# Four score banks a unit on VectorE instead of two in the second layer, and values ahead of background work, in a four-layer attention kernel

## The chip, the cores and the metric

The kernel runs on one core of a Trainium2 chip, as one launch. The metric is the device time of a launch in microseconds (us). Five engines matter here: TensorE (PE in the profile; its weight loads are PEld), ScalarE (ACT), VectorE (DVE), GpSimd (POOL) and SyncE (SP), which only issues DMAs. Each works through its own queue strictly in order; a semaphore makes one wait for another. PSUM has eight banks of 128 x 512 float32 words.

## What is computed

Four attention layers follow one another on a sequence of 2048 rows of 640 values, with 32 heads of 20 values:

```python
x = x + A(layernorm(x))   # window: key j counts for query i only if 0 <= i-j < 256
x = x + B(layernorm(x))   # every query sees every key, no mask
x = x + A(layernorm(x))
x = x + B(layernorm(x))
# A and B: softmax(q @ k.T * 20**-0.5 [masked in A]) @ v, heads joined, @ wo
```

The code counts layers from 0: layers 0 and 2 are windowed (A), layers 1 and 3 are full (B). "The second layer" is layer 1.

## The kernel before

**Units.** The queries go in four chunks of 512 (`c`), the heads in eight groups of four (`g`). A unit is one layer, chunk and group. Its scores come in banks: one bank is one block of 128 keys (`kc`) against 512 queries for one of the four heads (`j`). A full-attention unit has 16 x 4 = 64 banks, a windowed one has 12 smaller ones. Units of the four layers are interleaved in one list: the four windowed units of layer 2 that follow a chunk of layer 1 stand between units of the next chunk of layer 1. Layer 1's chunk 0 is cut into four parts by keys, because its keys appear only as layer 0 goes on.

**Tiles (ticks).** The main loop puts two or three banks together to a tile. One turn of the loop, a tick, handles one tile `t` and issues in this order:

1. TensorE: the scores of tile `t` (line 1318) into one of two sets of PSUM banks, 0 to 2 for even tiles, 3 to 5 for odd ones. So scores of `t` wait until ScalarE has read tile `t-2`.
2. ScalarE: one exponential over the tile (line 1349), written as bf16 to a `pt` buffer.
3. Background work (`pump`, then `keep_clock`): normalisation, projections, output projections, the division by the softmax sums (`t_tail`), all as generators that are advanced by a credit per tick. All of their matmuls go through the helper on line 300 or its neighbours, into PSUM bank 6 (from the end of the first stage on the only bank left for them; before it, bank 5 as well), and VectorE empties the bank (lines 323, 568, 1053, 1071, 1092). `keep_clock` fills up with matmuls whose result nobody reads (`masks,ident`), so that each tick has a least amount of TensorE work: 1.76 of its units for three banks, less in proportion for fewer.
4. TensorE: the values, that is `pt` times V of a tile two ticks back (three for windowed units), accumulated in PSUM bank 7 (line 1382). At a unit's end VectorE copies bank 7 out (line 864 and its neighbours).
5. VectorE: one step or so of the side work (below), paid from a credit of its own.
6. VectorE and GpSimd: the masks of the tile before, for windowed units (lines 1431 and 1421).

The "first stage" is what `state["early"]` marks. It ends with the last part of layer 1's chunk 0, at 433 us in the profile.

**Side work.** A few banks of a full unit don't go to ScalarE: `u.aside` lists them, and VectorE computes their exponentials with a polynomial (`t_side`). Per bank it reads the scores from PSUM as scaled integers (line 920), then per pair of banks it runs five operations on 128 x 1024 values (lines 925, 931, 936, 944, 948). In layer 1 the side bank is scored by TensorE as the third bank of a tile that then holds only two banks for ScalarE, so the number of banks that TensorE scores in a tile stays three. At the unit's end its pair is multiplied with V on line 1391. Layer 3 does the same for six banks a unit, with the scores in bank 6 (line 914) rather than in a tile. Layer 1's side work has buffers in `raw_o`, which chunk 0 no longer needs, and two outgoing buffers for finished pairs.

**Where side banks stand.** The list of tiles up to layer 3's second chunk is made ahead of the loop. Side bank number `n` of a unit may stand at the earliest `3 * n` tiles after the unit's first one, which makes tiles 0 and 3 for two banks.

Of the kernel before, what the change touches and what calls it, by code (L numbers as in the profile page):

```python
# [22 lines left out]
NT = S // P  # L23
# [3 lines left out]
NC = S // C  # L27
# [9 lines left out]
E1, E0, EA, EB = 6.520200689873914e-06 * FIX, 0.7855486869812012, -1.118533968925476, 1.5344765186309814  # L37
KA = 18
SIDE_RATE = 1.2
QA = 4  # L40

PARTS = {
# [6 lines left out]
def kernel(  # L49
# [201 lines left out]
    def pump(credit, most):  # L251
        state["credit"] = min(state["credit"] + credit, most)
        floor = 0.0
        while True:
            t = choose(state["credit"] <= floor)
            if t is None:
                break
            state["credit"] -= advance(t)
            if t not in tails:
                floor = 0.6  # L260
# [390 lines left out]
    def keep_clock():  # L651

        while cool():
            t = choose(False)
            if t is not None and state["credit"] > -0.5:
                state["credit"] -= advance(t)
                continue
            b = min(mfree, key=mfree.get)
            if state["early"] and mfree[b][0] > state["tick"]:
                break  # L660
            if mfree[b][0] > state["tick"] - (0 if state["early"] else 0):
                state["owed"] += 1
                state["heat"] += 1.0
            else:
                unread(b)
        spare = state["heat"] + state["carry"] - state["least"]
        state["carry"] = min(max(spare, 0.0), 3.0)
        state["heat"] = 0.0
# [5 lines left out]
    class Unit:  # L674
        def __init__(self, l, c, g, part=None):
            self.l, self.c, self.g, self.part = l, c, g, part
            self.windowed = l % 2 == 0
            self.aside = ()
            if self.windowed:
                sets = [(m, b0, subs, j) for m, b0, subs in window_banks(c) for j in range(4)]  # L680
            else:

                if c > 0 and (l, c, g) != (3, 1, 0):
                    self.aside = tuple((NT - 1, j) for j in ((2, 3) if l == 1 else range(4)))
                    if l == 3 and (c, g) != (NC - 1, G - 1):
                        self.aside += ((NT - 2, 0), (NT - 2, 1))
                k0, k1 = key_blocks(l, part)
                sets = [
                    (None, 0, [(kc, 0, 4, 0)], j) for kc in range(k0, k1) for j in range(4)
                    if (kc, j) not in self.aside  # L690
                ]
            n = len(sets)
            self.banks = [
                (self, j, m, b0, subs, i < 4, i >= n - 4 + len(self.aside), i == n - 1)
                for i, (m, b0, subs, j) in enumerate(sets)
            ]
# [506 lines left out]
    with tc.manual_schedule():  # L1203
# [9 lines left out]
        woven = index[1, 0, 0, PARTS[1][0]]  # L1213

        banks = [b for u in units for b in u.banks]
        tiles = []
# [4 lines left out]
        while n < last_layer:  # L1221
            size = 2 if len(tiles) % 2 and narrow(banks[n][0]) else 3
            u = banks[n][0]
            at = placed.setdefault(id(u), [])
            extra = []
            if (
                len(at) < len(u.aside) and banks[n + 1][0] is u
                and len(tiles) >= 3 * len(at) + (at or [0])[0]
            ):
                kc, j = u.aside[len(at)]  # L1230
                extra = [(u, j, "side", 0, [(kc, 0, 4, 0)], False, False, False)]
                at.append(len(tiles))
                size = 2
            for b in banks[n : n + size]:
                starts.setdefault(id(b[0]), len(tiles))
            tiles.append(banks[n : n + size] + extra)
            n += size
# [20 lines left out]
        def rate(t):  # L1258

            if t >= len(tiles):  # L1260
                return 0.45
            u = tiles[t][0][0]
            if index[u.l, u.c, u.g, u.part] < woven:
                return 1.2
            done, r = 0.0, 0.6 if state["early"] else 0.3
            for task in todo:
                done += max(task.left, 0.0)
                if task.need < len(units):
                    r = max(r, done / max(starts[id(units[task.need])] - t - 16, 1))
            return min(1.1 * r, 1.0 if u.l == 0 else 0.9)  # L1270

        last_tick[0] = len(tiles)
        wide_pt = 0
# [7 lines left out]
        while ended is None or t < ended + 8:  # L1281
# [3 lines left out]
            if t < len(tiles) or banks:  # L1285
# [67 lines left out]
                    i = k  # L1353
                for i, b in enumerate(cur):
                    pts.append((t, pt, i, b))
                state["least"] = (1.76 if state["unit"] >= woven else 1.0) * n_b / 3
                state["floor"] = 0.9 if state["unit"] >= index[1, 1, 0, None] else 0.0
                load_ahead()
                r = rate(t)
                pump(r, r + 0.1)  # L1360
                keep_clock()
            else:
                ended = t if ended is None else ended
                pump(2.0, 2.0)
# [1 line left out]
            for n in range(2 if n_b == 0 or t > closed + 1 else 0):  # L1366
# [30 lines left out]
                if end:  # L1397
# [2 lines left out]
                    closed = t  # L1400
                    break

            if n_b:
                side["credit"] = min(side["credit"] + ((SIDE_RATE if state["unit"] < index[3, NC - 1, 0, None] else 1.1) if side["late"] else 0.4), 1.3)
                side_step(False)

            if t > 0 and masked is not None:
# [71 lines left out]
```

## Time and profile before

| | us |
|---|---|
| median of three runs | 2222.56 |
| the three runs | 2214.69, 2222.56, 2223.66 |
| the profiled execution | 2214.42 |
| its span, first instruction to last | 2212.7 |
| ScalarE busy in it | 2139.9 (97%) |
| TensorE busy (matmuls, ends modelled) | 1919.8 (87%) |
| VectorE busy | 1199.8 (54%) |
| GpSimd busy | 482.5 (22%) |
| mean granted TensorE clock | 0.996 |

Busy time is the union of an engine's instructions. Two instructions that follow one another on ScalarE overlap in the records (the second starts reading while the first still writes), so the mean duration of one is longer than the time from its start to the next start; where an engine is the bound, it is this pitch that counts. In the groups of instructions the columns are line, engine, operation, tiles, shape and count, then busy time, mean ns of one, and idle time of the engine just before them with what ended it. The list of waits has, for each engine and line, what it waited for, the total in us, the number of times and the longest. The table by stretches has, for each engine, its busy time in the stretch and its number of instructions.

Four stretches of the profile are used below: up to 478 us (layers 0 and 1, chunk 0), 478 to 1272 us (layer 1's chunks 1 to 3 with the windowed units of layer 2 between them), 1272 to 1570 us (layer 3's first chunk, first part, with the last windowed units, then its second part) and 1570 us to the end (layer 3).

### The profile page before, as it was taken

Reading aid. Unit: us, or ns where it says so; the run is one execution under the profiler, and the core shown is the slowest. Engines: PE = TensorE matmul, PEld = TensorE weight load, DVE = VectorE, ACT = ScalarE, POOL = GpSimd, SP = SyncE. Lnnn points to the kernel's source line nnn. Section 1 sums busy time; section 2 is a strip of 40 time slices with the busy share of each in tenths; the row PEclk is TensorE's granted clock in tenths of the full one; section 3 lists DMA queues with packets and bytes.
Section 4 is the critical chain, followed back from the end, with each engine's and each line's share of the span. In section 5 each row is a group of like instructions: output and inputs, shape, how many; then the busy total and the mean of one; then the engine's idle time right before and its main releaser. Section 6 shows DMA issues by size and latency. Waiting matters only on the chain.

```text
span 2212.7 us, 70085 instructions
## 1 busy us (share of the span) xinstructions
PE 1919.8 (87%) x30415; PEld 756.1 (34%) x30415; DVE 1199.8 (54%) x2190; ACT 2139.9 (97%) x1734; POOL 482.5 (22%) x950
## 2 busy tenths in 40 slices
PE   8889998988888888888888888888888888888888
PEld 4444443333333333333333433342332222222222
DVE  6656564434445454444554533532467767767774
ACT  7889899999999999999999999999999999999998
POOL 6664545200231114301143112511000000000000
PEclk9999999999999999999999999999999999999999
DMA  6233323421211223112230123122121111111100
GB/s 200 74 99 91 88 81 93 102 78 45 74 41 33 71 60 97 33 34 66 66 104 24 48 72 100 36 57 63 54 62 35 32 32 44 32 32 35 49 24 16
DMA packets 88404, 137.09 MB, mean 62 GB/s; under 512 B 20766, under 2 KB 63486, under 8 KB 88094
## 3 DMA queue, kind: packets, MB, share of 16 engines
q1 hardware_dynamic: 68878, 79.43, 13.0%
q0 software_dynamic: 19216, 53.17, 8.1%
q8 instruction: 238, 3.90, 0.7%
q14 instruction: 72, 0.59, 0.1%
HBM read 99.52 MB, written 27.79 MB: 58 GB/s over the span
## 4 chain that ended last, share of the span: by engine, by line
ACT 52%; PE 21%; issue 18%; DVE 6%; DMA 1%; POOL 1%; ACTq 0%; DVEq 0%; POOLq 0%
ACT pt L1349 51%; PE ps L300 12%; PE ps L1318 5%; PE ps L1382 2%; DVE on L1092 1%; DVE st L323 1%; DVE pt L1431 1%; DMA wqk<-in_B_wqkv_dram 1%; PE ps L1088 1%; PE ps L437 0%; DVE on L864 0%; DVE x_sb L568 0%; DVE raw_o L920 0%; POOL pt L1421 0%; DVE xnT L323 0%
## 5 line engine op out<-in xcount | busy, mean ns | idle before, releaser
L1349 ACT ACTIVATE pt<-ps 128x1536 bf16<-128x1536 f32 (+2 forms) x1657 | 2104.3, 1456 | 41.8 <-PE ps L1318 32.1
L1318 PE MATMUL ps<-qt,kt 32*128 32x512 bf16 x3960 | 544.6, 384 | 91.4 <-ACT pt L1349 82.9
L300 PE MATMUL ps<-masks,ident 128*32 128x512 bf16 x5844 | 510.2, 387 | 117.8 <-ACT pt L1349 68.5
L1382 PE MATMUL ps<-pt,vt 128*21 128x512 bf16 x3908 | 397.6, 383 | 1.9 <-issue 1.0
L1318 PEld LDWEIGHTS <-kt 32*128 32x128 bf16 x3960 | 163.4, 91 | 546.4 <-issue 531.0
L300 PEld LDWEIGHTS <-ident 128*32 128x32 bf16 x5844 | 165.3, 94 | 349.9 <-issue 336.7
L1421 POOL TENSOR_SCALAR_AFFINE_SELECT pt<-pt 128x256 bf16<-128x256 bf16 (+2 forms) x505 | 213.8, 445 | 189.0 <-ACT pt L1349 183.5
L300 PE MATMUL ps<-xnT,wqk 128*32 128x512 bf16 x3320 | 224.6, 383 | 15.7 <-DVE st L323 4.0
L323 DVE CAST st<-ps 128x512 bf16<-128x512 f32 x134 | 92.7, 692 | 234.0 <-PE ps L300 230.4
L920 DVE TENSOR_SCALAR xnT<-ps 128x512 int32<-128x512 f32 x136 | 93.6, 688 | 134.1 <-PE ps L914 124.6
L300 PE MATMUL ps<-wop,on 128*32 128x320 bf16 x3712 | 159.8, 301 | 7.1 <-DVE x_sb L568 4.0
L1431 DVE TENSOR_TENSOR pt<-pt,masks 128x512 bf16<-128x512 bf16 (+4 forms) x267 | 112.4, 436 | 96.8 <-ACT pt L1349 94.6
L1382 PEld LDWEIGHTS <-vt 128*21 128x21 bf16 x3912 | 104.8, 91 | 126.1 <-issue 94.1
L300 PEld LDWEIGHTS <-on 128*32 128x32 bf16 x5760 | 113.5, 95 | 74.2 <-issue 51.1
L1318 PE MATMUL ps<-qa,ka 32*128 32x384 bf16 (+2 forms) x1408 | 114.7, 275 | 27.5 <-ACT pt L1349 24.4
L568 DVE TENSOR_TENSOR x_sb<-x_sb,ps 128x320 bf16<-128x320 bf16 x120 | 58.3, 486 | 146.8 <-PE ps L300 146.6
L300 PE MATMUL ps<-wv,xnT 128*32 128x320 bf16 x2560 | 115.2, 301 | 8.3 <-DVE on L1092 2.2
L1092 DVE TENSOR_TENSOR on<-on,ps 128x512 bf16<-128x512 bf16 x128 | 86.3, 684 | 57.9 <-PE ps L1088 56.7
L300 PEld LDWEIGHTS <-wqk 128*32 128x32 bf16 x3320 | 77.1, 95 | 114.4 <-issue 61.9
L864 DVE CAST on<-ps 128x512 bf16<-128x512 f32 x112 | 77.0, 687 | 57.0 <-PE ps L1391 32.6
L536 POOL DMA_DIRECT2D k_d<-st x75 | 43.0, 573 | 233.2 <-DVE st L323 223.2
L404 POOL TENSOR_SCALAR rstd<-mv 128x4 f32<-128x4 f32 x15 | 3.7, 248 | 382.6 <-DVE mv L391 374.4
(100 smaller groups left out, 1537.5 us busy)
## 6 DMA issues: line engine op xcount, KB each, us to landing
vt<-v_d SPq DMA_DIRECT2D x48, 336.0 KB
kt<-k_d SPq DMA_DIRECT2D x192, 80.0 KB
wqk<-in_B_wqkv_dram POOLq DMA_DIRECT2D x80, 160.0 KB, 3.4
wqk<-in_A_wqkv_dram POOLq DMA_DIRECT2D x70, 160.0 KB, 3.6
k_d<-st POOLq DMA_DIRECT2D x75, 128.0 KB, 2.6
q_d<-st POOLq DMA_DIRECT2D x75, 128.0 KB, 2.2
qt<-q_d SPq DMA_DIRECT2D x384, 20.0 KB
v_d<-vs POOLq DMA_DIRECT2D x16, 336.0 KB, 3.0
```

The source lines that it names most:

```text
L300: nc.tensor.matmul(out_[r], lhsT=lhsT[:, r], rhs=rhs, start=start, stop=stop)
L323: nc.vector.tensor_copy(out=out_, in_=in_)
L536: nc.gpsimd.dma_start(out=dst, in_=staging.pop())
L568: nc.vector.tensor_tensor(out=xv, in0=had, in1=yp, op=ALU.add)
L864: nc.vector.tensor_copy(out=oT, in_=op)
L920: V.tensor_scalar(out=xi.bitcast(I32)[:, i * C : (i + 1) * C], in0=side["psum"], scalar1=SCALE * LOG2E * FIX, scalar2=-127.0 * FIX, op0=AL ...
L1092: nc.vector.tensor_tensor(out=oT, in0=oT, in1=zb, op=ALU.mult)
L1318: nc.tensor.matmul(sp[:, i, col * P : (col + qn) * P], lhsT=u.k(kc, j), rhs=u.q(j, q0, qn), start=True, stop=True,)
L1349: nc.scalar.activation(out=pt[:, i:k, b0 * P :], in_=sp[:, i:k, b0 * P :], func=ACT.Exp, scale=SCALE,)
L1382: nc.tensor.matmul(op[32 * j : 32 * j + VW, q0 * P : (q0 + qn) * P], lhsT=u.v(kc, j), rhs=pg[:, i, col * P : (col + qn) * P], start=(first ...
L1421: nc.gpsimd.affine_select(out=v, in_=v, compare_op=ALU.is_gt if later else ALU.is_ge, fill=0.0, base=0, pattern=[[0, k - i], [-1 if later ...
L1431: nc.vector.tensor_tensor(out=pt_[:, i:k, cols], in0=pt_[:, i:k, cols], in1=mv_, op=ALU.mult)
```

## The change

Three edits stand in the diff. Layer 1's later chunks list four banks a unit as aside, not two: all four heads of the last key block. They may stand at tiles 0, 3, 9 and 12 of the unit at the earliest, and the credit that paces the side work there rises from 0.4 to 0.7 a tick; layer 3's numbers stay. The background work of a tick is put into a function, `background`, that is called at the old place in the first stage only; from its end on it is called after the values of the tick.

```diff
+SIDE_AT = (0, 3, 9, 12)
...
                 if c > 0 and (l, c, g) != (3, 1, 0):
-                    self.aside = tuple((NT - 1, j) for j in ((2, 3) if l == 1 else range(4)))
+                    self.aside = tuple((NT - 1, j) for j in range(4))
...
-                and len(tiles) >= 3 * len(at) + (at or [0])[0]
+                and len(tiles) >= SIDE_AT[len(at)] + (at or [0])[0]
...
+        def background(t, n_b):
+
+            state["least"] = (1.76 if state["unit"] >= woven else 1.0) * n_b / 3
+            state["floor"] = 0.9 if state["unit"] >= index[1, 1, 0, None] else 0.0
+            r = rate(t)
+            pump(r, r + 0.1)
+            keep_clock()
...
-                state["least"] = (1.76 if state["unit"] >= woven else 1.0) * n_b / 3
-                state["floor"] = 0.9 if state["unit"] >= index[1, 1, 0, None] else 0.0
                 load_ahead()
-                r = rate(t)
-                pump(r, r + 0.1)
-                keep_clock()
+                if state["early"]:
+                    background(t, n_b)
             else:
                 ended = t if ended is None else ended
                 pump(2.0, 2.0)
...
+            if n_b and not state["early"]:
+                background(t, n_b)
             if n_b:
-                side["credit"] = min(side["credit"] + ((SIDE_RATE if state["unit"] < index[3, NC - 1, 0, None] else 1.1) if side["late"] else 0.4), 1.3)
+                side["credit"] = min(side["credit"] + ((SIDE_RATE if state["unit"] < index[3, NC - 1, 0, None] else 1.1) if side["late"] else 0.7), 1.3)
                 side_step(False)
```

The omitted stretch ahead of the last edit holds the loop over the values (line 1366 on in the kernel before).

## The prediction

> **What bounds the kernel now.** I read the busy times first, then a table of four stretches, then ScalarE's timeline, then what TensorE waited for.
>
> ```profile
> PE 1919.8 (87%) x30415; PEld 756.1 (34%) x30415; DVE 1199.8 (54%) x2190; ACT 2139.9 (97%) x1734; POOL 482.5 (22%) x950
> ```
>
> ScalarE is the bound, and the table by stretches says where:
>
> ```profile
> 430.00:478.00 48.00, 40.25 (x562) 15.02 (x563) 13.67 (x25) 47.98 (x37) 9.08 (x13) 1.00 0.30 83
> 478.00:1272.00 794.00, 680.17 (x10967) 278.13 (x10959) 384.86 (x745) 786.19 (x620) 169.60 (x317) 1.00 0.21 58
> 1272.00:1570.00 298.00, 254.74 (x4075) 105.65 (x4068) 102.41 (x212) 293.95 (x219) 71.44 (x129) 0.99 0.24 67
> 1570.00:2200.00 630.00, 549.23 (x7051) 170.95 (x7050) 440.51 (x609) 626.77 (x466) 0.00 (x0) 1.00 0.12 35
> ```
>
> After the length come busy PE, PEld, DVE, ACT, POOL. In 478:1272, where the side banks change, ScalarE is busy 786.2 of 794 us (99%) and VectorE 384.9 (48%). So work taken from ScalarE shortens the stretch, if TensorE delivers scores fast enough. The price of a bank comes from the pitch, start to start, not from durations, since exponentials overlap:
>
> ```profile
> 1492.23 39.06 ACT L1349 ACTIVATE pt<-ps 128x1536 bf16<-128x1536 f32 x29 [0.39 <-PE ps L1318]
> ```
>
> ```profile
> 552.10 1.11 ACT L1349 ACTIVATE pt<-ps 128x1024 bf16<-128x1024 f32 x1
> ```
>
> ```profile
> 553.00 1.55 ACT L1349 ACTIVATE pt<-ps 128x1536 bf16<-128x1536 f32 x1
> ```
>
> Columns: start, length, then the group. 29 three-bank exponentials back to back take 39.06 us; less one duration (1.55) that is 28 pitches of 1.34. Undisturbed ones in the records are 1.333 apart. The two-bank one starts 0.90 before its successor; undisturbed ones give 0.905. A bank taken from a tile saves 1.333 - 0.905 = **0.428 us**, less than the 482 ns by which the mean durations differ (1553 and 1071).
>
> Third, TensorE's slack: its waits in 478:1272.
>
> ```profile
> PE ps L1318 <- ACT pt L1349: 55.4, 170, 0.7
> PE ps L300 <- DVE st L323: 14.2, 47, 0.6
> PE ps L300 <- ACT pt L1349: 10.4, 28, 0.7
> PE ps L300 <- DVE on L1092: 7.9, 16, 0.8
> ```
>
> It waited 65.8 us (55.4 + 10.4) for ScalarE to free score banks. That is what it can give when ScalarE gets faster: 8% of the stretch, so TensorE is a close second. The waits for VectorE (st, on and smaller ones) are losses in its queue.
>
> **Part 1, two more banks a unit.** There are 24 such units (3 chunks x 8 groups), so 48 banks move. The instruction order of the changed kernel agrees: 50 three-bank exponentials fewer, 47 two-bank ones more, two wide ones of 2048 columns more in layer 3 (pitch 1.757). ScalarE: 50 x 1.333 - 47 x 0.905 - 2 x 1.757 = **-20.6 us**, all in 478:1272 but for the wide ones.
>
> Added to VectorE: 48 x 0.69 (line 920) and, for each of 24 pairs, 0.69 + 0.70 + 1.22 + 1.21 + 0.68 (lines 925, 931, 936, 944, 948) = 33 + 108 = 141 us, which takes its stretch to (385 + 141) / 773 = 68%. That lies beside ScalarE as long as VectorE's queue empties bank 6 and the side banks in time. TensorE: scores and values are the same in number; 17 unread fillers (of 1461) go, since a two-bank tile asks for less; the granted clock is 1.00 in 478:1272 now, and I price so few at nothing. POOL and SP get no instruction more.
>
> What a short tile costs: TensorE has 0.43 us less for that tick. In 478:1272 pitches exceed the undisturbed ones by 20.3 us, of which 17.7 us lie in a two-bank tile or the three tiles after it (sums over the records). That would be 0.37 us for each of today's 48, nearly the whole saving. But these tiles stand at a unit's start, where the tails of the unit before run and values catch up two groups a tick. The new ones stand at tiles 9 and 12. Over the 24 units TensorE's waits for ScalarE per three tiles, from the unit's first side bank, are on average 0.18, 0.24, 0.32, 0.38, 0.50, 0.50, 0.38 us: from the ninth tile on 1.76, against 0.86 for two short tiles. Bounds: 0 (all absorbed) to +17.7 (like today's). I take **+5**, 0.1 each, nearer to the mid-unit row, since that is where they stand; not zero, because single units have under 0.5 there.
>
> Third suspect, the pace: in the changed order each second pair is finished about 6 tiles ahead of its values (line 1391), so nothing waits there. Side banks are read in time today: of 48 reads, 19 found VectorE idle, and no wait of TensorE on line 920 shows in this stretch.
>
> VectorE's longer queue: records of background between scores and values hold 34.3 us of waits for VectorE in 144 of 451 cases in 478:1272. If they grow with VectorE's load (0.65 to 0.86 us a tile in the two orders, a third more), that is +11 us of TensorE's time, against 66 us of slack. Bounds: 0 to +11. I take **+2**, because most of it falls where TensorE would wait for ScalarE anyway.
>
> A rule that speaks against the part. In 478:1570, k_d's DMA issues on POOL took 0.56 us on average (30 with no side operation beside them) and 0.62, up to 1.03 (10 beside one). The Trainium skill (SBUF — State Buffer, Who interferes with whom) says that VectorE and GpSimd share a port pair, which a VectorE operation with two SBUF inputs or in a two-port mode holds for its whole length while the other blocks fully. By the row, twice the side work costs POOL 0.05 us on some ten issues more; by the rule each could wait up to a whole operation. POOL is 21% busy there, and I price it at nothing.
>
> **Part 2, values ahead of background.** From 433 us on. It adds no instruction. What stands behind the values is now the background; what stands behind a waiting background matmul is now only the next scores. Gain: a background matmul that waits for VectorE to empty bank 6 does so after the values (0.3 to 0.4 us later), so that part of the wait is filled. Cutting each wait by the length of the values behind it removes, from the records, 23.4 us of TensorE's time in 478:1272, 7.7 in 1272:1570 and 5.5 later. That is worth ScalarE's time only where it stood idle or late: 20.3 us in 478:1272, about 7 and 9 in the others; of the 33 single delays over 0.3 us after 478, 18 have VectorE waits of 0.4 or more in TensorE's queue just before. Bounds: 0 to -12 us (a third of 36). I take **-5**.
>
> Cost: values may now wait for their own masks or exponentials. Comparing, record by record, when each group's `pt` was ready with when the background ahead of it began, 12 of 893 groups would have waited, 5.2 us together (POOL masks 6, VectorE masks 5, 1.9 us of it at the very end). Bounds 0 to +5; I take **+1**. The copies of bank 7 now stand ahead of the background's on VectorE: a gain for the next unit's values, which start two ticks later anyway, at nothing. k_d's and q_d's DMAs on POOL leave up to 0.4 us later; loads are issued units ahead, at nothing.
>
> **Sum.** -20.6 + 5 + 2 - 5 + 1 = **-17.6 us**. Against the profiled execution: 2214.4 - 17.6 = 2196.8, span about 2195. The profile lies at the lower end of four executions (2214.42, 2214.69, 2222.56, 2223.66; mean 2218.8); from their mean I get **2201**.
>
> **Rivals.**
>
> (a) *TensorE becomes the bound in short tiles.* The new short tiles lose what today's lose, 17.7 us, and values ahead gives little: -20.6 + 17.7 - 2 = -5, so about 2214. For it: 87% busy TensorE, zero slack in some units' starts. Against: the slack at tiles 9 to 21.
>
> (b) *Slower: bank 6 behind VectorE.* The side steps of 1.22 us stand ahead of the copies that free bank 6; TensorE waits in order, and scores come late. The price passes the saving when the waits for VectorE exceed TensorE's remaining slack, 65.8 - 20.6 = 45 us, by 20.6; to be 11 us slower they must grow by about 77 us, over 0.5 us in each of the 144 cases that wait now. Then about 2230. For it: 141 us more on VectorE. Against: 1570:2200, where VectorE is busier still (440.5 of 630, 70%) and ScalarE stays at 626.8; though there is less background there.
>
> (c) *Values ahead is worth more than I take.* The whole -12, short tiles absorbed: -20.6 - 12 + 3 = -30, about 2189.
>
> (d) *The edit doesn't move the work.* The built order excludes this: it has 50 three-bank exponentials fewer and 48 operations like line 920's more, and the values now stand ahead of the background in most ticks.
>
> **How the numbers follow.** Forecast (2193 to 2209) 0.65; (a) 0.15; (c) 0.12; (b) 0.08. The range leaves out (b) and the far end of (c): **2186 to 2216**. A measurement can tell about 0.5% (11 us) from no change: faster means below 2211.4. The forecast and (c) lie below it, and a little of (a): faster **0.80**; the rest of (a): same **0.13**; (b): slower **0.07**.
>
> **What would show it.** In 478:1272 (then some 18 us shorter) ScalarE still 98 to 99% busy, 104 or so two-bank exponentials, about 96 operations on line 920's successor; TensorE's wait for ScalarE down from 65.8 towards 50; its waits for VectorE not above today's, as values ahead cuts them by more than the load adds; 1570:2200 shorter by 1 to 3 us. Wrong if ScalarE's idle time before exponentials grows by over 10 us (a), or if TensorE's waits for VectorE double (b).

## The result, and the profile after

| | before | after |
|---|---|---|
| median of 22 runs each, us | 2218.03 | 2227.67 |
| lowest to highest | 2214.63 to 2224.43 | 2219.20 to 2234.89 |
| the profiled execution | 2214.42 | 2221.95 |
| its span | 2212.7 | 2219.7 |
| mean granted TensorE clock | 0.996 | 0.991 |

The ratio is **1.004, with an interval of [1.0031, 1.0049]**: 9 us slower, where 17.6 us less were forecast. The forecast, its range and its sign were wrong; the time lies nearest to rival (b), 2230.

The busy line of the page after, and its costliest group:

```profile
PE 1928.6 (87%) x30347; PEld 746.5 (34%) x30347; DVE 1334.8 (60%) x2358; ACT 2125.6 (96%) x1733; POOL 486.2 (22%) x950
L1358 ACT ACTIVATE pt<-ps 128x1536 bf16<-128x1536 f32 (+2 forms) x1654 | 2086.6, 1433 | 59.2 <-PE ps L1327 47.9
```

The work moved as the diff says: VectorE is busy 135 us more, ScalarE 14 us less, and yet the span is longer. ScalarE now stands idle 47.9 us waiting for scores (line 1327). The same group before, with 32.1 us (line 1318):

```profile
L1349 ACT ACTIVATE pt<-ps 128x1536 bf16<-128x1536 f32 (+2 forms) x1657 | 2104.3, 1456 | 41.8 <-PE ps L1318 32.1
```

The stretches of after from 478 us on:

```profile
478.00:1272.00 794.00, 682.64 (x10818) 270.03 (x10815) 506.31 (x895) 766.32 (x615) 168.48 (x310) 0.98 0.21 56
1272.00:1570.00 298.00, 256.10 (x4116) 103.50 (x4113) 113.08 (x228) 295.17 (x222) 76.14 (x136) 1.00 0.26 70
1570.00:2200.00 630.00, 548.25 (x7062) 170.00 (x7060) 442.58 (x609) 626.97 (x465) 0.00 (x0) 1.00 0.13 36
```

In 478:1272 ScalarE is busy 766.3 us (96.5%; 786.2 before), VectorE 506.3 (384.9) and the clock is 0.98 (1.00). The other stretches are nearly as they were. What TensorE waited for in 478:1272 after the change:

```profile
PE ps L1327 <- ACT pt L1358: 37.5, 115, 0.6
PE ps L301 <- DVE st L324: 12.8, 20, 1.7
PE ps L301 <- DVE on L1093: 11.8, 31, 0.9
PE ps L301 <- DVE x_sb L569: 7.3, 16, 1.6
PE ps L301 <- ACT pt L1358: 6.6, 22, 0.7
...
PE ps L438 <- DVE xn L418: 5.7, 4, 2.1
PE ps L301 <- DVE rT L1072: 5.4, 12, 1.5
```

Its waits for ScalarE fell from 65.8 to 44.1 us. Of its waits for VectorE those on `st` became fewer (47 to 20), but the longest went from 0.6 to 1.7 us, and those on `x_sb` (2.6 us before), `xn` (none) and `rT` (1.9) grew. ScalarE's own waits in the same stretch, first before, then after:

```profile
ACT pt L1349 <- PE ps L1318: 6.1, 18, 0.8
```

```profile
ACT pt L1358 <- PE ps L1327: 24.2, 58, 1.3
```

Four times as much: 18 us, nearly all that the shorter exponentials gave.

**Floor and excess.** To compare runs I took "layer 1's stretch" between two fixed VectorE copies of bank 7 (the 64th and the 120th of 160, about 493 to 1410 us). Its *floor* is what ScalarE would take without a delay: each exponential of the stretch times the undisturbed pitch of its width (1.333 and 0.905 us for three and two banks, and likewise for the narrow ones). The *excess* is what the pitches exceed it by. A delay of over 0.05 us is put to *clock* if it overlaps a time of half clock, to *VectorE* if TensorE waited for VectorE for at least half of it between 2 us before the start of the exponential ahead and the time when the late one was due, and else to *busy* TensorE. The rule is mine and splits mixed cases crudely: with only the 2 us right before the late start, VectorE / clock / busy would be 17.8 / 9.7 / 21.6 after and 12.3 / 3.1 / 8.9 before. Floor, excess and the clock's part don't depend on that choice. Floor and excess meet the stretch to within 1 us, its edges. A drop is an unbroken time at half clock. All times are us:

| | before | after |
|---|---|---|
| start of the stretch | 493.1 | 494.5 |
| layer 1's stretch | 914.1 | 918.4 |
| of it floor | 888.8 | 868.3 |
| of it excess | 24.7 | 50.1 |
| excess by VectorE / clock / busy | 13.4 / 3.1 / 7.8 | 26.9 / 9.7 / 12.5 |
| drops of the clock in it, us at half clock | 3, 10.2 | 7, 23.9 |
| the rest, to the span's end | 805.6 | 806.9 |

The floor fell by 20.5 and the excess rose by 25.4. The other 2.7 us of the spans' 7.0 lie outside: 1.4 in the first stage, whose code is the same and whose length scatters from 493 to 499 us over the runs of this study, and 1.3 after the stretch.

The timed runs follow the granted clock. Of after's 22 runs, those at 0.982 to 0.985 took 2230.0 to 2234.9 us and those at 0.988 to 0.993 took 2219.2 to 2225.2; the median clock is 0.987. Runs of the kernel before, timed beside the experiments, have a median of 0.993 to 0.995. At the same clock the two kernels take the same time: about 2222 us at 0.991 and 2219 at 0.993. So what after loses goes with a lower clock; which of the two brings the other, these numbers don't say.

### The profile page after: what moved, and what is told of

It reads as the page before. It is cut to its first block, busy times and chain, and to the rows that moved or that the text cites. A ratio compares the mean times of both kernels' runs of the same rounds, so it can differ in the third digit from the quotient of the medians.

```text
span 2219.7 us, 70181 instructions
## 1 busy us (share of the span) xinstructions
PE 1928.6 (87%) x30347; PEld 746.5 (34%) x30347; DVE 1334.8 (60%) x2358; ACT 2125.6 (96%) x1733; POOL 486.2 (22%) x950
## 3 DMA queue, kind: packets, MB, share of 16 engines
q1 hardware_dynamic: 68878, 79.43, 13.5%
## 5 line engine op out<-in xcount | busy, mean ns | idle before, releaser
L1358 ACT ACTIVATE pt<-ps 128x1536 bf16<-128x1536 f32 (+2 forms) x1654 | 2086.6, 1433 | 59.2 <-PE ps L1327 47.9
L1327 PE MATMUL ps<-qt,kt 32*128 32x512 bf16 x3960 | 553.2, 385 | 75.5 <-ACT pt L1358 66.8
L301 PE MATMUL ps<-masks,ident 128*32 128x512 bf16 x5776 | 504.4, 386 | 121.5 <-ACT pt L1358 63.2
L1388 PE MATMUL ps<-pt,vt 128*21 128x512 bf16 x3852 | 388.4, 388 | 1.1 <-ACT pt L1358 1.1
L301 PEld LDWEIGHTS <-ident 128*32 128x32 bf16 x5776 | 175.7, 94 | 303.5 <-issue 274.9
L1388 PEld LDWEIGHTS <-vt 128*21 128x21 bf16 x3864 | 96.2, 89 | 248.7 <-issue 245.0
L301 PEld LDWEIGHTS <-on 128*32 128x32 bf16 x5760 | 119.8, 95 | 67.6 <-issue 33.8
L1327 PE MATMUL ps<-qa,ka 32*128 32x384 bf16 (+2 forms) x1408 | 114.9, 276 | 25.1 <-ACT pt L1358 21.2
L865 DVE CAST on<-ps 128x512 bf16<-128x512 f32 x112 | 77.0, 688 | 68.7 <-PE ps L1397 44.6
L301 PEld LDWEIGHTS <-wqk 128*32 128x32 bf16 x3320 | 83.5, 96 | 102.8 <-issue 46.8
L1093 DVE TENSOR_TENSOR on<-on,ps 128x512 bf16<-128x512 bf16 x128 | 86.3, 684 | 47.4 <-PE ps L1089 40.4
L921 DVE TENSOR_SCALAR raw_o<-ps 128x512 int32<-128x512 f32 x96 | 66.1, 689 | 51.1 <-PE ps L1327 49.2
```

The source lines that it names most:

```text
L301: nc.tensor.matmul(out_[r], lhsT=lhsT[:, r], rhs=rhs, start=start, stop=stop)
L865: nc.vector.tensor_copy(out=oT, in_=op)
L921: V.tensor_scalar(out=xi.bitcast(I32)[:, i * C : (i + 1) * C], in0=side["psum"], scalar1=SCALE * LOG2E * FIX, scalar2=-127.0 * FIX, op0=AL ...
L1093: nc.vector.tensor_tensor(out=oT, in0=oT, in1=zb, op=ALU.mult)
L1327: nc.tensor.matmul(sp[:, i, col * P : (col + qn) * P], lhsT=u.k(kc, j), rhs=u.q(j, q0, qn), start=True, stop=True,)
L1358: nc.scalar.activation(out=pt[:, i:k, b0 * P :], in_=sp[:, i:k, b0 * P :], func=ACT.Exp, scale=SCALE,)
```

## The experiments

Three theories stood against one another, under the letters that the expectations use. **V**: VectorE's 141 us of new work make TensorE wait for bank 6. **T**, the short tiles themselves: after a tile of two banks the next scores are due 0.43 us earlier and come late. **C**: fewer fillers let the granted clock drop. The first two runs also ask after **O**: the new order itself costs. Each run's ratio is to the kernel before, with its interval; "stretch" is layer 1's, as floor + excess. Line numbers move by a few between kernels.

### Each part alone

`e1_values_only` keeps two banks and the old pace; `e2_banks_only` keeps the old place of the background:

```diff
-SIDE_AT = (0, 3, 9, 12)
+SIDE_AT = (0, 3)
...
-                    self.aside = tuple((NT - 1, j) for j in range(4))
+                    self.aside = tuple((NT - 1, j) for j in ((2, 3) if l == 1 else range(4)))
...
```

```diff
-                if state["early"]:
-                    background(t, n_b)
+                background(t, n_b)
...
-            if n_b and not state["early"]:
-                background(t, n_b)
```

> Values ahead of background alone; two banks a unit at tiles 0 and 3 and the old pace, as before. Theory V (VectorE's longer queue makes TensorE wait in order, and the clock drop follows from such waits): 3 to 6 us faster than before, excess of ScalarE's pitches in layer 1's later chunks below 22 us, granted clock there as before (2 drops or fewer). Theory O (values ahead of background itself costs): slower than before by 5 us or more. Theory T (TensorE can't feed the short tiles) says nothing here: no more short tiles than before, so 0 to -6 us.

> Four banks a unit with the new places and pace, background at its old place. Theory V: TensorE's waits for VectorE are as large as in the changed kernel or larger, since nothing fills them: 5 to 15 us slower than before, and slower than the changed kernel by 0 to 6 us. Theory O: 10 us faster than before, since the order was what cost. Theory T: within 5 us of the changed kernel.

e1: 1.0001 [0.9991, 1.0012], stretch 913.3 = 888.8 + 24.4. e2: 1.0003 [0.9992, 1.0015], stretch 915.3 = 868.3 + 46.5. Values ahead alone does nothing (-0.8 us), and four banks alone break even: the floor's 20.5 us are there, and the excess eats them. Together they are worse than either. With four banks, values ahead costs 3.1 us of stretch (918.4 against 915.3), and by the timed ratios 1.0040 - 1.0003, that is 8 us; most of the 8 goes with the clock (median 0.992 in e2's runs, 0.987 in after's). For e1, T's 0 to -6 us is nearest; V's gain and O's loss don't show. For e2 none of the three came true by the timed ratio.

That e1 gains nothing has a plain reason in its list of waits. Values ahead was to fill TensorE's waits for VectorE, and they were not filled: in 478:1272 they add up to 36.4 us in e1, 34.3 before. Those on `st` halved, those on `on` grew (7.9 before):

```profile
PE ps L301 <- DVE on L1093: 12.7, 29, 0.9
...
PE ps L301 <- DVE st L324: 7.0, 16, 0.8
```

### VectorE's work without the short tiles, and the short tiles without the work

`e3_second_pair_not_computed` keeps all four banks in their places, but the second pair's five operations aren't issued (its values use the first pair's result). `e7_second_pair_hardly_read` also reads only 8 of the second pair's 512 columns per bank. `e4_before_second_pair_twice` is the kernel before with the five operations done twice, at the changed kernel's pace.

```diff
+                if u.l == 1 and pair == 1:
+                    for cost in (0.7, 0.7, 1.2, 1.2, 0.7):
+                        yield cost
+                    side_out[id(u)].append(side_out[id(u)][0])
+                    continue
...
```

```diff
-                        out=xi.bitcast(I32)[:, i * C : (i + 1) * C], in0=side["psum"],
+                        out=xi.bitcast(I32)[:, i * C : i * C + w], in0=side["psum"][:, 0:w],
```

> The changed kernel, but in layer 1 VectorE leaves out the five operations of each unit's second pair (120 operations, 108 us) and the first pair's result is used twice, so part of the softmax isn't computed. ScalarE, TensorE and the pace are those of the changed kernel. Theory V: 12 to 22 us faster than the changed kernel (8 to 18 faster than before), no waits of TensorE over 1 us for xn or rT, two clock drops in layer 1's later chunks. Theory T: within 4 us of the changed kernel, since the short tiles stay. Theory C (fewer fillers in two-bank tiles let the clock drop): within 4 us, seven drops there.

> As e3 (second pair of layer 1 not computed, first pair's result used twice), and VectorE reads only 8 of the 512 columns of the second pair's banks, so nearly nothing of VectorE's added work is left, while ScalarE's and TensorE's tiles are those of the changed kernel. Layer 1's stretch was 909.1 us in e3, 914.1 before. Theory V: 901 us or less, excess of the pitches at tiles 9 to 15 of a unit below 5 us (15.6 in e3). Theory T: 906 to 910 us, that excess above 10 us.

> The kernel before (two banks, old order), but in layer 1 VectorE runs the five pair operations a second time on scratch, at the pace of the changed kernel: VectorE's load without any bank taken from ScalarE. Theory V: 10 to 25 us slower than before, with TensorE's waits for VectorE in layer 1's later chunks doubled from 33 us and more clock drops than two. Theory T and theory C: within 5 us of before, since no tile is shorter and no filler fewer.

| | ratio | stretch | floor + excess | VectorE / clock / busy |
|---|---|---|---|---|
| e3 | 0.9996 [0.9982, 1.0009] | 909.1 | 868.3 + 40.8 | 21.2 / 6.8 / 12.5 |
| e7 | 0.9975 [0.9964, 0.9987] | 910.0 | 868.3 + 41.7 | 20.0 / 8.9 / 12.4 |
| e4 | 1.0020 [1.0010, 1.0029] | 919.2 | 888.8 + 29.9 | 16.7 / 4.8 / 8.2 |

So computing the second pair costs 918.4 - 909.1 = **9.3 us** (1.0040 - 0.9996, 10 us, by the timed ratios). Reading its banks costs nothing by the stretch (e7's is not shorter than e3's); the timed ratio is 0.2% lower with intervals that just overlap, so a few us may hang on it. The same load beside two short tiles costs 5.1 in the old order (e4). But 40.8 - 24.7 = **16.1 us** of excess remain without that load. That this is not VectorE's load alone shows in e3's list of TensorE's waits, in its two largest groups for VectorE:

```profile
PE ps L301 <- DVE on L1098: 11.8, 31, 0.9
PE ps L301 <- DVE st L324: 8.4, 19, 0.8
```

None of these is above 0.9 us (smaller groups reach 1.5), and `st` is below the 14.2 of before; over the whole stretch, short waits included, TensorE waited 53.4 us for VectorE, against 49.3 before. And yet ScalarE waits two and a half times as long as before (6.1), two thirds of what it does in after:

```profile
ACT pt L1363 <- PE ps L1332: 16.1, 42, 1.3
```

Where the excess lies says more. In the two-bank tiles of the side banks and up to three tiles behind each, the pitches exceed the floor by 17.5 us before (48 such tiles). In after it is 13.9 us at the two old places and 17.0 at the two new ones, and in e3 13.5 and 15.7. So the new short tiles alone hold 15.7 us in e3, close to the 16.1 in all. The 9.3 us of the second pair lie elsewhere: only 1.7 of them there, and 7.3 in the tiles four to six behind a short one (11.2 us in after, 3.9 in e3, 0.2 before).

The timelines that follow show how a short tile loses time. Before, a wait of 0.57 us on the division's copy (`on`), among three-bank tiles:

```profile
1169.67 5.49 ACT L1349 ACTIVATE pt<-ps 128x1536 bf16<-128x1536 f32 x4
...
1172.14 0.40 PE L300 MATMUL ps<-masks,ident 128*32 128x512 bf16 x4 [0.57 <-DVE on L1092]
...
1173.12 0.39 PE L1318 MATMUL ps<-qt,kt 32*128 32x512 bf16 x3
```

The scores end at 1173.5, the next exponential is due at 1169.67 + 3 x 1.333 = 1173.67, and ScalarE's chain of four isn't broken. After, the same wait behind a new short tile:

```profile
1008.89 2.37 ACT L1358 ACTIVATE pt<-ps 128x1536 bf16<-128x1536 f32 x2 [0.22 <-PE ps L1327]
...
1009.81 0.69 DVE L1093 TENSOR_TENSOR on<-on,ps 128x512 bf16<-128x512 bf16 x1 [0.22 <-PE ps L1327]
...
1010.55 0.40 PE L301 MATMUL ps<-masks,ident 128*32 128x512 bf16 x4 [0.56 <-DVE on L1093]
...
1011.12 0.37 PE L1327 MATMUL ps<-qt,kt 32*128 32x512 bf16 x1
...
1011.60 1.45 ACT L1358 ACTIVATE pt<-ps 128x1536 bf16<-128x1536 f32 x1 [0.35 <-PE ps L1327]
```

The second of the two exponentials is the two-bank one; it starts at 1010.23, so its successor was due at 1011.14. The last scores end at 1011.49 and it starts at 1011.60: 0.46 us lost. TensorE doesn't even have to wait for anything:

```profile
1100.41 0.86 PE L301 MATMUL ps<-wv,xnT 128*32 128x320 bf16 x20
1100.45 0.69 DVE L921 TENSOR_SCALAR raw_o<-ps 128x512 int32<-128x512 f32 x1
1101.20 0.39 PE L1327 MATMUL ps<-qt,kt 32*128 32x512 bf16 x3
...
1101.70 1.45 ACT L1358 ACTIVATE pt<-ps 128x1536 bf16<-128x1536 f32 x1 [0.42 <-PE ps L1327]
```

Here 0.8 us of background matmuls ahead of the scores are enough. Over the stretch, the median time from the end of a tile's scores to the start of its exponential is 0.51 us where the tile before had three banks (0.49 after), and 0.11 where it had two, in both kernels. TensorE works ahead by two sets of banks only, so a short tile's 0.43 us come off this lead.

### The copies that free bank 6

`e16_after_narrow_copies` and `e17_before_narrow_copies` let VectorE's copies `st`, `x_sb` and `on` from bank 6 handle 64 columns after the first stage, with four banks and with two (`x_sb`, in layers 1 and 2, is changed alike):

```diff
-        evac(dst(), pq)
+        w = C if state["early"] else 64
+        evac(dst()[:, 0:w], pq[:, 0:w])
...
-        nc.vector.tensor_tensor(out=oT, in0=oT, in1=zb, op=ALU.mult)
+        w = C if state["early"] else 64
+        nc.vector.tensor_tensor(out=oT[:, 0:w], in0=oT[:, 0:w], in1=zb[:, 0:w], op=ALU.mult)
```

> The changed kernel, but after the first stage VectorE's copies that free bank 6 for TensorE do only 64 columns: the projections' copy to st (64 of 512, from fixed zeroed buffers), the product with the softmax sums (64 of 512) and, in layers 1 and 2, the residual sum (64 of 320). So parts of q, k, the normalisation and the residual are left out; TensorE and ScalarE do all they did. To be read against e17. If TensorE's waits for VectorE over bank 6, uncovered in short tiles, carry the loss: layer 1's stretch here 14 to 20 us shorter than in e17, excess of the pitches 30 or less. If TensorE's own work in the short ticks carries it: at most 8 us shorter than e17, excess 35 or more.

> The kernel before with the same narrow copies as e16. Either way its layer 1 stretch is 5 to 12 us shorter than 914.1, with the part of the excess that follows waits for VectorE down from 13.4 us to 5 or less; the floor stays 888.8.

| | ratio | stretch | floor + excess | VectorE / clock / busy |
|---|---|---|---|---|
| e16, four | 0.9948 [0.9929, 0.9966] | 897.8 | 868.3 + 29.6 | 8.4 / 6.2 / 14.5 |
| e17, two | 0.9955 [0.9938, 0.9973] | 904.7 | 888.8 + 15.7 | 3.5 / 3.7 / 8.1 |

With short copies four banks are 6.9 us of stretch better than two, where they are 4.3 worse with the full ones. So **11 us** of the difference hang on the copies that free bank 6. The timed ratios agree on that turn: 0.0040 worse becomes 0.0007 better, 10 us, though the two intervals here overlap. The remaining 29.6 - 15.7 = 13.9 us of excess don't: 6.4 of them fall to busy TensorE, 4.9 to VectorE, 2.5 to the clock (10.4, 1.0 and 2.5 with only the 2 us right before). ScalarE's waits, e16 and then e17:

```profile
ACT pt L1364 <- PE ps L1333: 12.9, 33, 1.1
```

```profile
ACT pt L1355 <- PE ps L1324: 2.1, 8, 0.5
```

Neither theory alone accounts for it. A short tile takes the lead away, and then whatever delays TensorE (a copy of VectorE's, its own background, a clock drop) reaches ScalarE.

### Fillers and the clock

`e5_full_fillers` gives a short tile the least TensorE work of three banks, `e10_no_fillers_near_short_tiles` gives a short tile and the next none, and `e6_rstd_six_ticks` gives GpSimd six ticks, not two, for the normalisation's `rstd`:

```diff
-            state["least"] = (1.76 if state["unit"] >= woven else 1.0) * n_b / 3
+            state["least"] = (1.76 if state["unit"] >= woven else 1.0) * (n_b + state.pop("side", 0)) / 3
...
+                    state["side"] = 1
```

```diff
+            if state.get("side", 0) > 0:
+                state["side"] -= 1
+                state["heat"] = 0.0
+                return
...
+                    state["side"] = 2
```

```diff
-        yield ("wait", 2)
+        yield ("wait", 2 if state["early"] else 6)
```

> The changed kernel, with the least amount of TensorE work in a two-bank tile asked for as if it had three banks, so that no filler goes. Layer 1's stretch is taken between two fixed copies of bank 7 (918.4 us in the changed kernel, 914.1 before). Theory C (fewer fillers let the clock drop): 5 to 10 us shorter, three clock drops or fewer in it instead of seven. Theory T (TensorE can't give the short tiles their time): 2 to 6 us longer. Theory V (late results of VectorE): within 2 us.

> The changed kernel without unread fillers in the tick of a two-bank tile and the one after (114 fillers fewer of 1444); background stays where it is. Theory T: layer 1's stretch 4 to 12 us shorter than 918.4, the lead of scores over the exponential after a two-bank tile above the 0.10 us of the changed kernel. Theory C: longer, with more than seven clock drops. Theory V: within 3 us.

> The changed kernel, with six ticks instead of two between GpSimd's 1/sqrt and VectorE's use of it after the first stage, so that VectorE doesn't stand waiting for GpSimd with the transposes behind it. Theory V: layer 1's stretch 3 to 8 us shorter than 918.4, no wait of TensorE over 0.5 us for xn, three to four clock drops fewer than seven in it. Theory T: within 2 us. Theory C: the drops stay.

| | ratio | stretch | excess | VectorE / clock / busy | drops, us at half clock |
|---|---|---|---|---|---|
| e5 | 1.0043 [1.0024, 1.0063] | 918.5 | 50.2 | 23.3 / 10.7 / 15.5 | 5, 23.9 |
| e10 | 1.0016 [1.0002, 1.0030] | 915.8 | 47.4 | 22.1 / 16.7 / 8.2 | 9, 37.5 |
| e6 | 1.0056 [1.0035, 1.0077] | 919.6 | 51.1 | 27.5 / 5.7 / 17.1 | 3, 10.2 |

C falls as the cause of the loss: the fillers back (e5) change nothing, and none at all near short tiles (e10) is a little better. Fewer fillers do come with more half clock (e10: 37.5 us, after 23.9). What e10 takes from busy TensorE (4.3) comes back as clock (7.0). e6 was aimed at a chain that the timeline of after shows:

```profile
539.72 1.17 DVE L937 SCALAR_TENSOR_TENSOR raw_o<-raw_o 128x1024 f32<-128x1024 f32 x1
...
539.90 1.04 POOL L405 TENSOR_SCALAR rstd<-mv 128x4 f32<-128x4 f32 x1 [83.38 <-DVE mv L392]
...
541.02 2.03 POOL L408 TENSOR_TENSOR rstd<-rstd,nhalf 128x4 f32<-128x4 f32 x1
...
543.08 0.16 DVE L411 SCALAR_TENSOR_TENSOR nmr<-mv,rstd 128x4 f32<-128x4 f32 x1 [0.94 <-POOL rstd L408]
...
543.90 0.46 PE L438 MATMUL ps<-ident,xn 128*32 128x128 bf16 x20 [2.14 <-DVE xn L418]
...
544.80 1.45 ACT L1358 ACTIVATE pt<-ps 128x1536 bf16<-128x1536 f32 x1 [1.33 <-PE ps L1327]
```

GpSimd's `rstd` takes 1.04 us beside a side operation (0.19 without one), VectorE waits for it, TensorE waits 2.14 us for `xn`, ScalarE stands idle for 1.33, and at 545.3 the clock drops. It looks like the culprit; but with six ticks the waits on `xn` and four of the seven drops are gone and the stretch is no shorter. TensorE got to other delays instead: its waits on `xnT` in 478:1272 went from 2.0 to 9.9 us.

### Place and number of the short tiles

`e11_tiles_0_5_10_15` spreads them, `e12_spread_and_no_fillers` joins that with e10's edit, `e8_no_background_in_short_tiles` issues no background and no filler in a short tile's tick, `e18_e8_in_old_order` is e8 with the background ahead of the values, and `e9_no_side_banks` is the kernel before without any side bank in layer 1.

```diff
-SIDE_AT = (0, 3, 9, 12)
+SIDE_AT = (0, 5, 10, 15)
```

```diff
         def background(t, n_b):
 
+            if state.pop("side", False):
+                return
...
                     n_b -= 1
+                    state["side"] = True
```

```diff
-                if c > 0 and (l, c, g) != (3, 1, 0):
+                if l == 3 and c > 0 and (l, c, g) != (3, 1, 0):
...
```

> The changed kernel with the side banks at tiles 0, 5, 10 and 15 instead of 0, 3, 9 and 12. Theory T: what is lost goes by the number of two-bank tiles, not by their place, as each needs the next scores at once: within 4 us of 918.4. If it is the pile of short tiles close together that exhausts TensorE's lead: 5 to 10 us shorter.

> e10 and e11 together, the best guess at a version that beats both kernels. Theory T: layer 1's stretch 6 to 14 us shorter than 918.4 (904 to 912), the whole 2 to 10 us faster than the kernel before. Theory C: slower than the changed kernel by clock drops.

> The changed kernel, but a tick of layer 1 with a two-bank tile has neither background work nor fillers; the background is done in the ticks after. Theory T: layer 1's stretch 6 to 14 us shorter than 918.4, the excess of the pitches at tiles 9 to 20 down from 25 us to 15 or less. Theory V: within 3 us. Theory C: longer, with more clock drops than seven.

> Four banks a unit at the changed kernel's places, no background and no fillers in the ticks of two-bank tiles (as e8), and the background ahead of the values as before. From e2 (1.2 us longer than before in layer 1's stretch, 3 us shorter than the changed kernel) and e8 (5.4 us shorter than the changed kernel): layer 1's stretch 908 to 913 us, the whole 2 to 6 us faster than the kernel before. If values ahead is what lets e8 gain: 914 us or longer.

> The kernel before with no side bank in layer 1 at all: 48 exponentials of two banks become three-bank ones, 20.5 us more for ScalarE by the pitches, and VectorE and TensorE's two-bank ticks are relieved. Theory T (a two-bank tile returns little, because the next tile's scores are not there earlier): layer 1's stretch 2 to 8 us longer than 914.1, and the excess of the pitches about 15 us lower than before's. If only the new places lose time: 15 to 20 us longer.

| | ratio | stretch | floor + excess | VectorE / clock / busy | drops, us at half clock |
|---|---|---|---|---|---|
| e11 | 1.0028 [1.0016, 1.0040] | 916.9 | 868.3 + 48.5 | 24.2 / 11.0 / 12.7 | 6, 23.9 |
| e12 | 1.0010 [0.9999, 1.0020] | 918.4 | 868.3 + 50.0 | 24.0 / 14.9 / 10.3 | 12, 51.2 |
| e8 | 0.9985 [0.9971, 0.9999] | 913.0 | 868.3 + 44.6 | 20.2 / 16.1 / 7.5 | 6, 44.4 |
| e18 | 1.0040 [1.0025, 1.0055] | 920.0 | 868.3 + 51.4 | 24.9 / 19.7 / 5.9 | 7, 44.4 |
| e9 | 1.0037 [1.0023, 1.0052] | 926.5 | 908.9 + 16.8 | 7.2 / 6.0 / 3.6 | 3, 10.2 |

The place hardly matters (e11: 1.5 us of stretch less than after). e12, meant to beat both kernels, does not; its clock is at half for 51.2 us. What e8 changes helps: with no background behind a short tile the lead after it is 0.30 us, not 0.11, the stretch is 5.4 us shorter than after's, a little under the 6 to 14 expected, and the result is the best version of this study that computes everything, 0.15% faster than before and only just clear of it. It needs the new order: in the old one (e18) the same edit takes 7.0 us of stretch more, against what was expected. The lead is 0.31 us there too and the time at half clock the same, so a longer lead alone doesn't bring the gain, and what else does stays open. e9 shows that the return diminishes. The first two banks took 20.1 us from the floor and added 7.9 to the excess, 12.4 us of stretch gained, more than expected; the second two took 20.5 and added 21.8 in the old order (e2) and 25.4 in the new. Without any side bank ScalarE hardly waits:

```profile
ACT pt L1350 <- PE ps L1319: 2.5, 5, 0.9
```

### Side banks in bank 6

If the short tile is the trouble, the side bank can be scored in PSUM bank 6, as layer 3 does, so that every tile for ScalarE has three banks: `e13_four_banks_by_bank_6`, `e14_two_banks_by_bank_6`, and `e15_four_by_bank_6_old_order`, which is e13 with e2's edit. The core of the edit:

```diff
-                len(at) < len(u.aside) and banks[n + 1][0] is u
+                u.l == 3 and len(at) < len(u.aside) and banks[n + 1][0] is u
...
-                    t % 2 and side["late"] and side["gen"] is not None and side.get("at") == "bank"
+                    (t % 2 or not side["late"]) and side["gen"] is not None and side.get("at") == "bank"
```

> The changed kernel, but layer 1's four side banks a unit are scored into PSUM bank 6 between background work, as layer 3 does it, so that ScalarE's tiles keep three banks and none is short (tiles also end where full and windowed units meet; ten weight buffers, not eight). ScalarE loses the same 48 banks more than before. If the short tile's missing lead is the cause: excess of the pitches in layer 1's stretch 50 in the changed kernel, here 25 to 36, the stretch 895 to 905 us, the whole 10 to 20 us faster than the changed kernel. If VectorE's round trips and bank 6 are the cause: excess 45 or more, since bank 6 is now shared further, the stretch 912 us or longer.

> As e13 with two side banks a unit, as before, so VectorE's load is that of the kernel before. If the short tile's lead is the cause: excess 15 to 19 us (16.8 with no side bank, 24.7 before), the stretch 904 to 909 us. If bank 6 is: excess 25 or more, the stretch 914 us or longer.

> As e13 with the background ahead of the values as in the kernel before. From e1 (values ahead alone: 0.8 us shorter in layer 1) and e2 against the changed kernel (3 us longer with it): within 3 us of e13 either way.

| | ratio | stretch | floor + excess | VectorE / clock / busy | drops, us at half clock |
|---|---|---|---|---|---|
| e13 | 1.0242 [1.0219, 1.0264] | 965.5 | 865.8 + 99.5 | 19.0 / 60.5 / 18.8 | 11, 64.9 |
| e14 | 1.0018 [1.0006, 1.0030] | 916.3 | 887.3 + 28.8 | 8.4 / 0 / 19.4 | 0, 0 |
| e15 | 1.0250 [1.0224, 1.0276] | 969.0 | 865.8 + 102.3 | 27.3 / 64.8 / 9.3 | 12, 68.3 |

The intended comparison failed for four banks: the one bank left for background is then shared with 96 side banks, the projections seem to come late, and TensorE waits for the windowed units' queries. From e13's list of TensorE's waits in 478:1272:

```profile
PE ps L1333 <- DMA qa<-q_d: 22.5, 14, 4.8
```

The clock drops in such waits, so my rule books most of them as clock. e14 has no drop and little VectorE excess, and still no gain: by my rule 19.4 of its 28.8 us are busy TensorE. It lands where it was expected if bank 6 were the cause (25 or more, 914 us or longer), so doing without short tiles gained nothing in this form, whose side banks share bank 6 with the background. These three say nothing on whether four banks could pay with a bank of their own.

## Why the prediction was wrong, step by step

**What bounds the kernel: half right.** ScalarE was the bound, and TensorE "a close second" with 65.8 us of waits. But that sum was taken for a stock to draw on. It was made of some 200 waits of at most 0.7 us, and with two sets of banks little of it can be carried over to the tick that follows a two-bank tile.

**ScalarE's saving: right.** -20.6 forecast, -20.5 in the floor. The floor is counted with the same pitches, so what the runs add is that they hold: the undisturbed exponentials in layer 1's stretch of after stand 1.331 and 0.904 us apart.

**Short tiles, +5 ("nearer to the mid-unit row, since that is where they stand"): the step that failed most.** With the second pair not computed the excess rose by 16.1 us, 0.34 for each of the 48 new short tiles, near the far bound of 0.37 (+17.7) that today's short tiles gave and that I put down to a unit's start. In after itself the new places hold 17.0 us, in mid-unit. Place was the wrong explanation, and spread to tiles 0, 5, 10 and 15 they cost nearly as much. The average slack per three tiles (1.76 us from the ninth tile on) was the wrong row; the lead behind a short tile, 0.11 us, is in the trace of before as well.

**VectorE's queue, +2: too small, inside its bounds.** Computing the second pair costs 9.3 us (bounds 0 to 11). "Most of it falls where TensorE would wait for ScalarE anyway" was wrong: 7.3 us of it come up four to six tiles behind a short one. Beside two short tiles, in the old order, the same load costs 5.1.

**Values ahead, -5 and +1: wrong.** The part alone moves the stretch by -0.8 and the time by nothing (1.0001). The step that failed is that the waits would be filled: 23.4 us of TensorE's time were to go from 478:1272, and its waits for VectorE there went from 34.3 to 36.4 us (e1). With four banks it costs 3.1 us of stretch and 8 us of time; what in the new order does it I haven't separated. It isn't the order as such: with no background in short tiles the new order is the better one (e8 against e18, 12 us by the timed ratios).

**Fillers at nothing: right** (e5). **The clock, priced at nothing with them: wrong.** It fell from 1.00 to 0.98 in 478:1272, and its part of the excess rose from 3.1 to 9.7 us, though not for want of fillers. **GpSimd's port at nothing: wrong in the row, right in the sum.** `rstd` on GpSimd went from 0.19 us in five of six cases in layer 1 before to 1.04 or 0.51 us in six of six after (six of six in e2, one in e3, none in e8), as the Trainium skill (SBUF — State Buffer, Who interferes with whom) warns of an operation that holds the shared port pair; I had looked at DMA issues alone. Taking the resulting wait away gained nothing (e6).

**The signs that the prediction named.** ScalarE's idle time grew by 18 us, over the 10 that were to speak for rival (a). TensorE's waits for VectorE over layer 1's stretch rose from 49.3 to 70.5 us, not to double, so (b)'s own condition wasn't met, though its time was nearly reached. (a) and (b) were given as alternatives with 0.15 and 0.08; they came together, and each was weighed against a slack that the other was using too.

In sum, on layer 1's stretch: -20.5 + 16.1 + 9.3 = +4.9, against +4.3 measured. The 16.1 and 9.3 are the whole growth of the excess, parted by e3, so this is no test of them; the 0.6 us are the edges, and what the new order costs with four banks is inside the two. Still open: how the 13.9 us that remain with narrow copies divide between TensorE's own work, VectorE and the clock, since taking fillers or background away turned busy time into clock drops (e10, e12), and why the granted clock is lower after: the medians lie 9.6 us apart, the profiled executions 7.5, the stretches 4.3, and the timed runs' part beyond the profile goes with the clock. After's runs scatter over 15.7 us, before's over 9.8, and the profiled ones are near the lower end of both.

## What to carry to other kernels

When the bound engine works a small ring of buffers that a nearly busy engine fills, price a shortened step by what such steps lose in the trace today (17.7 us for 48 here, and 17.0 for the 48 new ones), not by the filler's total waits. Work taken from the bound engine in equal portions doesn't give equal returns: the first pair gained 12.4 us of stretch here, and the second lost 1.2 in the old order and 4.3 in the new one, so measure what the last portion brought before adding another. And a wait that looks like the culprit in a timeline may only be the first of two: take it away before believing it.

## What the runs showed of the hardware

**The clock drops on a grid.** Drops to half clock within the stretch last 3.41 us or a whole multiple of it (up to 17.07, in e15), and in the records of each execution their starts lie whole multiples of 3.413 us apart (545.33, 722.83 and 763.78 in after: 52 and 12 steps). Over layer 1's stretch in the 20 traces, the steps at full clock by TensorE's busy share in them:

| busy share of the step | steps | followed by a drop |
|---|---|---|
| under 0.55 | 58 | 51 |
| 0.55 to 0.67 | 130 | 36 |
| 0.67 to 0.75 | 449 | 15 |
| 0.75 and more | 4586 | 2 |

All but one of after's seven drops follow a single wait of TensorE of 1.0 to 2.1 us, in a kernel where it is busy 87% of the time. The Trainium skill (TensorE: Matmul & The Clock Gate, What's actually happening) states a free-running window of 3413 ns, which agrees; its advice (Why this matters for your kernels) to avoid idle gaps above some 3 us is too lax for what these runs show.

**Small GpSimd operations beside VectorE's two-input ones.** `rstd` (128 x 4 values) took 0.19 us alone and 0.51 or 1.04 beside a side operation (in the timeline above it ends at 540.94, the side operation at 540.89); its power 1.04 and once 2.03. In the other direction the side step on line 926 took 0.69 us alone and up to 1.02 beside DMA issues of GpSimd's.
